# Hash attention and Fourier mixing on one core: values of pairs 5 to 15 fetched by GpSimd through a table of row numbers

## The chip, the core and the metric

The kernel runs on one core of one Trainium2 chip. The metric is the device time of one execution in microseconds. Names in the profile: PE is TensorE (matrix products), PEld its weight loads, DVE is VectorE, ACT is ScalarE, POOL is GpSimd and SP is SyncE, which here only issues DMA transfers. [...]

## The reference, cut to what matters

```python
# q, k, v: (4, 8, 768, 64) float32; proj: (64, 6)
q_bits = (einsum('bhsd,dk->bhsk', q, proj) > 0); k_bits likewise
mask = q_bucket[:, :, :, None] == k_bucket[:, :, None, :]     # buckets: 6 bits as a number
scores = where(mask, q @ k^T / 8, -1e9)
attn = softmax(scores)                                        # per batch and head, 768 x 768
x = (attn @ v) -> (B, S, H*D)                                 # (4, 768, 512)
u = x + real(fft(fft(x, axis=1), axis=2))
un = (u - mean(u)) / sqrt(var(u) + 1e-6)
out = u + relu(un @ w_ch1) @ w_ch2                            # 512 -> 2048 -> 512
```

## The kernel before, in words

There are 4 batches with 8 heads each. The heads are worked in pairs of two: pair n (0 to 15) holds heads 2t and 2t+1 of batch b, with n = 4b + t. Four constants are used below: P = 128 partitions, NT = 6 blocks of 128 rows in a sequence of 768, D = 64 and NPAIR = 4.

**Attention.** For each pair there are six steps, one per block c of 128 keys. In a step, weigh forms the transposed scores in PSUM (L893), ScalarE takes the exponential into the tile pk (L897), VectorE sets the pairs of different buckets to zero (L903) and adds up the denominators in acc (L988). One step later values multiplies by the values (L914): the weights loaded into TensorE are a block of 128 rows and 64 columns of vn, the tile of values of this pair. In vn (128 partitions, 768 columns) block c of head h stands in columns (2c + h) * 64 and up; partition p holds row 128c + p of the sequence. There are two such tiles in turn, so the values of pair n + 1 go where those of pair n - 1 were, and they can be fetched when the last product of pair n - 1 is done.

**Loads.** load(n) fetches q, k and v of a pair. It is called for pair n + 1 at the start of pair n, before the pair's first step. In the kernel before all of it is issued on SyncE's queue (for pair 0 partly on ScalarE's): for pairs 1 to 15, q takes 8 transfers, k takes 4 and v takes 2, one for each head (L562), each with 768 pieces of 256 bytes.

**Mixing.** mix(b) is the Fourier transform as products with constant tables (L1086, L1115), and then mlp7(b), the two linear layers with seven products in place of eight (L1390 for the first, L1270 for the second). The transposed u comes back through ScalarE (L1142); spread computes the mean and the variance of its rows on VectorE, and on GpSimd the scale rs (L1151 and L1152), with which VectorE later adds the second layer's products to the output (L1282). store sends the output from GpSimd's queue (L1024), for the last batch from SyncE's.

**Weights.** The weights come as 64-bit numbers and are made 32-bit on the chip by narrow, of which ScalarE does L647, L654 and L655, and VectorE L639, L643 and L652. The first layer's are fetched on SyncE's queue during batch 0. The second layer's are fetched on GpSimd's queue (L693, tile zraw) in 16 transfers of 512 KB into two buffers in turn, while the attention of batch 1 runs. From batch 1 on the first layer's blocks come back from a scratch tensor ad (L1363) and the second layer's from bd (L1275), on SyncE's queue.

**What sets the order.** Attention of batch b and the mixing of batch b - 1 are interleaved: after each step of attention(b) some steps of the generator mix(b - 1) are run. Up to the end of batch 0's attention the order of TensorE, VectorE, ScalarE and GpSimd is that of the program text (the block under tc.manual_schedule). From batch 1 on a planner sets the order on each engine: among the instructions whose operands are ready by its own modelled times it takes the one that stands earliest in the program, save for the chains of scores and values on TensorE, which behind() ties to each other with a higher rank. The load of pair 5 is called at the start of pair 4, which is the first pair of batch 1.

Of the kernel before, what the change touches and what calls it, by code (L numbers as in the profile page):

```python
# [13 lines left out]
I32 = mybir.dt.int32  # L14
# [6 lines left out]
P = 128  # L21
B, H, S, D = 4, 8, 768, 64
# [3 lines left out]
NT = S // P  # L26
NPAIR = H // 2
# [458 lines left out]
def _main(  # L486
# [13 lines left out]
    nc = tc.nc  # L500

    const = ctx.enter_context(tc.tile_pool(name="const", bufs=1))
# [11 lines left out]
    def wt(shape, dtype, tag, name, bufs=2):  # L514
        return work.tile(shape, dtype, tag=tag, name=name, bufs=bufs)
# [26 lines left out]
    def load(n, names="qkv", second=nc.sync):  # L542

        b, t = divmod(n, NPAIR)
        for nm in names:
            src = {"q": q, "k": k, "v": v}[nm]  # L550
            tag, bufs = ("vn", 2) if nm == "v" else ("qkn", 2)
            tl = wt([P, S], F32, tag, f"{nm}n{n}", bufs)
            nat[nm, n] = tl
            if nm == "v" or n == 0:
                tc_ = tl.rearrange("p (c h d) -> p c h d", c=NT, h=2)
                for h in range(2):
                    s = src[b, 2 * t + h]
                    s = (
                        s.rearrange("(p c) d -> p c d", c=NT) if nm == "q"
                        else s.rearrange("(c p) d -> p c d", p=P)  # L560
                    )
                    (second if h else nc.sync).dma_start(tc_[:, :, h, :], s)  # L562
                continue
            for i in range(4):
                s = src[b, 2 * t + i // 2, :, i % 2 * 32 : i % 2 * 32 + 32]
                d = tl[32 * i : 32 * i + 32]
                if nm == "k":
                    nc.sync.dma_start(
                        d.rearrange("p (j a) -> p j a", a=32),
                        s.rearrange("(j b) a -> b j a", b=32),  # L570
                    )
                else:
                    s = s.rearrange("(j b r) a -> r b j a", b=32, r=2)
                    d = d.rearrange("p (r j a) -> r p j a", r=2, a=32)
                    for r in range(2):
                        nc.sync.dma_start(d[r], s[r])

    load(0, "qk", nc.scalar)
    warm = const.tile([1, 1], F32, tag="warm", name="warm")
    nc.gpsimd.memset(warm, 0.0)  # L580
# [13 lines left out]
    own = const.tile([P, 2], F32, tag="own", name="own")  # L594
    nc.sync.dma_start(own, cn["own"].ap())
    load(0, "v")
    pj = const.tile([P, 32], F32, tag="pj", name="pj")
    nc.gpsimd.memset(pj, 0.0)
# [112 lines left out]
    def weights1():  # L711
# [11 lines left out]
        for i in range(arrival.depth):  # L723
            arrival.fetch(i)
            if i == 1:
                load(1)
# [826 lines left out]
def kernel(tc, *args):  # L1553

    cn = {n: tc.nc.inline_tensor(a, name="k_" + n) for n, a in _consts().items()}
    with ExitStack() as ctx:
        large = _main(ctx, tc, *args, cn)
    with tc.If(large > 0, preferred_fallthrough_block=False):
        _any_scores(tc, *args, cn)
# [34 lines left out]
```

## Time and profile before

| | |
|---|---|
| median of 2 runs | 1102.0 us (1101.22 to 1102.78) |
| the profiled execution | 1102.7 us, of which its span 1100.4 us |
| granted TensorE clock, mean | 0.994 |
| DMA: packets, bytes | 175,710, 103.13 MB |
| SyncE's hardware queue | 169,840 packets, 30.1% of 16 engines |
| GpSimd's software queue | 4,224 packets, 3.7% |
| instructions on GpSimd | 132 |

All times below are microseconds from the start of the span unless marked ns. A group row gives line, engine, operation, tiles (output <- inputs), number, busy time and mean. A row of waits gives who waited, for whom, the total time, how many times and the longest one. A row of a timeline gives start, duration, engine, line, operation and tiles, and in square brackets how long the engine had been idle and what ended this. DMA instructions on an engine's row last as long as the engine needs to issue them; the landing comes later, for vn 3.4 us (median) after the issue and for zraw fetches from GpSimd 4.0 us.

The attention of batch 0 takes the first 114 us or so; that of batch 1 lies between 124.8 and 447.9 us (first product of pair 4 to last of pair 7, with the mixing of batch 0 in between), batch 2 from there to 642.5, apart from an early start at 412.9, and batch 3 ends at 899.5. After that the rest of the mixing of batch 2 and that of batch 3 run alone.

### The profile page before, as it was taken

The numbers are of one execution on the slowest core, as the hardware profiler recorded it, in microseconds if no ns is written. First come the engines' busy times: TensorE is split into PE (matmuls) and PEld (weight loads), VectorE is DVE, ScalarE is ACT, GpSimd is POOL, SyncE is SP. The second block draws the span as 40 slices with busy tenths as digits, with TensorE's granted clock in tenths as the row PEclk, the third lists the DMA queues.
The fourth block names the chain that finished last, engine by engine and source line by source line (L and its number), as shares of the span: only waits on it lengthen the run. The fifth ranks groups of instructions, "written<-read, shape, count | busy, mean of one in ns | idle before, by whom it ended". The sixth has DMA issues, their size and how long they took to land.

```text
span 1100.4 us, 14144 instructions
## 1 busy us (share of the span) xinstructions
PE 1043.3 (95%) x4933; PEld 632.7 (57%) x4933; DVE 790.5 (72%) x1336; ACT 499.5 (45%) x1055; POOL 58.6 (5%) x132
## 2 busy tenths in 40 slices
PE   7989897999989999999999999999999999999996
PEld 3333353446744675545664576645674569768575
DVE  5899958878599977776767785965856785644353
ACT  6987555553276324454326433355315522340420
POOL 0000000002000020010000011001000002100000
PEclk9999999999999999999999999999999999999998
DMA  9755353451056161322154134213032205122301
GB/s 222 224 95 126 64 140 72 138 164 19 20 149 209 44 204 26 68 63 66 26 157 107 48 82 153 44 43 92 15 129 68 68 24 172 55 81 88 123 20 41
DMA packets 175710, 103.13 MB, mean 94 GB/s; under 512 B 129552, under 2 KB 162960, under 8 KB 175632
## 3 DMA queue, kind: packets, MB, share of 16 engines
q1 hardware_dynamic: 169840, 88.65, 30.1%
q0 software_dynamic: 4224, 13.11, 3.7%
q8 instruction: 41, 0.67, 0.2%
q10 hardware_dynamic: 1568, 0.39, 0.2%
q14 instruction: 37, 0.30, 0.1%
HBM read 81.14 MB, written 20.97 MB: 93 GB/s over the span
## 4 chain that ended last, share of the span: by engine, by line
PE 61%; DVE 11%; ACT 4%; DMA 2%; issue 2%; DVEq 0%; SPq 0%; ACTq 0%
PE o L1270 22%; PE h_p L1390 20%; PE oo L914 6%; PE sc L893 6%; DVE pk L903 3%; PE cs L1086 2%; DMA zraw<-in_moe_w_ch_dram 2%; PE A L1115 2%; PE B L1115 1%; DVE acc L988 1%; ACT rr L948 1%; DVE w L1282 1%; DVE h L1256 1%; PE bits L825 1%; PE un L1141 1%
## 5 line engine op out<-in xcount | busy, mean ns | idle before, releaser
L1270 PE MATMUL o<-w,h 128*128 128x256 f32 x1152 | 259.4, 382 | 1.2 <-ACT tq L1289 0.7
L1270 PEld LDWEIGHTS o<-w,h 128*128 128x128 f32 x1152 | 216.3, 190 | 43.6 <-issue 4.6
L897 ACT ACTIVATE pk<-sc 128x768 f32<-128x768 f32 x192 | 147.6, 809 | 78.4 <-PE sc L893 60.9
L1390 PE MATMUL h_p<-x,w 128*128 128x384 f32 x448 | 163.5, 495 | 3.2 <-ACT h L1412 1.5
L893 PE MATMUL sc<-qt,kt 64*128 64x384 f32 x768 | 155.7, 508 | 6.0 <-ACT pk L897 5.7
L914 PE MATMUL oo<-pk,vn 128*64 128x385 f32 (+1 forms) x768 | 155.3, 499 | 6.0 <-DVE pk L903 3.0
L903 DVE SCALAR_TENSOR_TENSOR pk<-qb,kb,pk 128x768 f32<-128x768 bf16 x132 | 129.0, 1012 | 30.2 <-ACT pk L897 30.1
L1390 PEld LDWEIGHTS h_p<-x,w 128*128 128x128 f32 x448 | 82.3, 190 | 71.0 <-ACT pk L897 5.4
L988 DVE TENSOR_TENSOR acc<-acc,pk 128x1536 f32<-128x1536 f32 (+1 forms) x72 | 105.7, 1482 | 7.2 <-ACT pk L897 6.7
L1390 PE MATMUL h_p<-w 128*128 128x384 f32 x288 | 105.5, 489 | 2.3 <-ACT w L1427 2.3
L914 PEld LDWEIGHTS oo<-pk,vn 128*64 128x64 f32 x768 | 49.1, 136 | 100.0 <-issue 69.3
L893 PEld LDWEIGHTS sc<-qt,kt 64*128 64x128 f32 x768 | 66.9, 188 | 51.3 <-issue 24.0
L1390 PEld LDWEIGHTS h_p<-w 128*128 128x128 f32 x288 | 53.7, 190 | 41.7 <-ACT w L1427 3.5
L1300 ACT COPY tq<-o 128x256 f32<-128x256 f32 x24 | 8.9, 372 | 105.1 <-PE o L1270 105.1
L1282 DVE SCALAR_TENSOR_TENSOR w<-o,rs,w 128x256 f32<-128x256 f32 x56 | 26.7, 478 | 41.6 <-PE o L1270 41.6
L1270 PE MATMUL o<-w 128*128 128x256 f32 x176 | 42.3, 383 | 1.3 <-DVE w L1282 1.3
L1416 DVE TENSOR_TENSOR h<-h 128x384 f32<-128x384 f32 x32 | 17.8, 556 | 33.1 <-ACT h L1415 33.1
L1289 ACT COPY tq<-o 128x256 f32<-128x256 f32 x24 | 8.9, 371 | 69.3 <-PE o L1270 69.2
L1270 PEld LDWEIGHTS o<-w 128*128 128x128 f32 x176 | 32.8, 190 | 8.8 <-DVE w L1282 2.9
L1423 DVE TENSOR_TENSOR h<-h 128x384 f32<-128x384 f32 x32 | 17.7, 553 | 27.0 <-ACT h L1422 27.0
L1024 POOL DMA_DIRECT2D out_dram<-w x30 | 16.4, 548 | 388.7 <-issue 293.2
L1086 PE MATMUL cs<-ch,z 128*128 128x128 f32 (+3 forms) x192 | 33.2, 324 | 3.0 <-DVE bt L829 1.9
(170 smaller groups left out, 1312.4 us busy)
## 6 DMA issues: line engine op xcount, KB each, us to landing
w<-ad SPq DMA_DIRECT2D x168, 128.0 KB, 2.0
w<-bd SPq DMA_DIRECT2D x42, 512.0 KB, 4.5
zraw<-in_moe_w_ch_dram POOLq DMA_DIRECT2D x16, 512.0 KB, 4.0
bd<-w SPq DMA_DIRECT2D x14, 512.0 KB, 3.9
vn<-in_v_dram SPq DMA_DIRECT2D x32, 192.0 KB, 3.4
qn<-in_q_dram SPq DMA_DIRECT2D x120, 48.0 KB, 2.4
kn<-in_k_dram SPq DMA_DIRECT2D x60, 96.0 KB, 3.4
zraw<-in_moe_w_ch_dram SPq DMA_DIRECT2D x8, 512.0 KB, 5.7
```

The costliest lines, as they stand in the source:

```text
L893: last[0] = nc.tensor.matmul(ps[:, h, 0:HALF], kt[rows, ks], qt[rows, qs], start=kb is not None, stop=True,)
L897: nc.scalar.activation(pk[:, g, :, 0:HALF], ps[:, :, 0:HALF], AF.Exp, scale=SCALE)
L903: nc.vector.scalar_tensor_tensor(w, qb[:, h].rearrange("p (g s) -> p g s", g=2), kb[:, h, c : c + 1], w, op0=ALU.is_equal, op1=ALU.mult,)
L914: nc.tensor.matmul(oos[g][h * D : (h + 1) * D, 0:w], nat["v", n][:, (2 * c + h) * D : (2 * c + h + 1) * D], pk[:, g, h, 0:w], start=(c == ...
L988: nc.vector.tensor_tensor(acc[:, g], (first if c == 1 else acc)[:, g], new[:, g], op=ALU.add,)
L1086: nc.tensor.matmul(ps[:, pc + 2 * lo : pc + 2 * hi - 1 : 2], z[:, cp, pc, par, t * P : (t + 1) * P], ch[:, cp, pc, lo:hi], start=(cp == 0) ...
L1115: nc.tensor.matmul(ps[:, cols], F[:, par, k, t, j * P : (j + 1) * P], sq[:, t, k, cols], start=(t == 0), stop=(t == 1),)
L1270: nc.tensor.matmul(ps, a[:, r], right7[i][:, r], start=start and r == 0, stop=r == HF // 2 - 1, skip_group_check=not start,)
L1282: nc.vector.scalar_tensor_tensor(t[:, cols], src, r, t[:, cols], op0=ALU.mult, op1=ALU.add)
L1390: nc.tensor.matmul(ps, left[:, k], right[i][:, k], start=start and k == 0, stop=k == 1, skip_group_check=not start,)
L1416: nc.vector.tensor_tensor(c21, c12, c21, op=ALU.add)
L1423: nc.vector.tensor_tensor(c22, c21, c22, op=ALU.add)
```

## The change

From pair 5 on (n > NPAIR) the values of a pair are no longer fetched by two transfers of SyncE. GpSimd issues twelve indirect transfers instead, one for each block c and head h. Each fetches 128 rows of 64 numbers; the row of v that goes to partition p is read from the column (2t + h) * 6 + c of a table rowid, to which the start of the batch is added as a constant. rowid has 128 partitions and 48 columns of 32-bit numbers; a single iota on GpSimd fills it at the start of the kernel, and column j holds 128j + p in partition p. So every row goes where it went before, and the rows are asked for in their old order. The loads of q and k, and of the values of pairs 0 to 4, stay.

```diff
             if nm == "v" or n == 0:
+                if n > NPAIR:
+                    rows = v.rearrange("b h s d -> (b h s) d")
+                    for j in range(2 * NT):
+                        c, h = divmod(j, 2)
+                        nc.gpsimd.indirect_dma_start(
+                            tl[:, j * D : (j + 1) * D], None, rows,
+                            bass.IndirectOffsetOnAxis(
+                                rowid[:, (2 * t + h) * NT + c : (2 * t + h) * NT + c + 1], 0
+                            ),
+                            element_offset=b * H * S * D,
+                        )
+                    continue
                 tc_ = tl.rearrange("p (c h d) -> p c h d", c=NT, h=2)
...
+    rowid = const.tile([P, H * NT], I32, tag="rowid", name="rowid")
+    nc.gpsimd.iota(rowid, pattern=[[P, H * NT]], base=0, channel_multiplier=1)
     load(0, "qk", nc.scalar)
     warm = const.tile([1, 1], F32, tag="warm", name="warm")
     nc.gpsimd.memset(warm, 0.0)
```

## The prediction, made before the result was known

> **What bounds the kernel now.** I read the page's busy table first, then the busy time by stage, then the waits of TensorE, then the transfers of values on SyncE's queue in order of time, and last the timeline of GpSimd around them.
>
> ```profile
> ## 1 busy us (share of the span) xinstructions
> PE 1043.3 (95%) x4933; PEld 632.7 (57%) x4933; DVE 790.5 (72%) x1336; ACT 499.5 (45%) x1055; POOL 58.6 (5%) x132
> ```
>
> TensorE is busy for 1043.3 of 1100.4 us, so all that any change can win is in the other 57 us; GpSimd is nearly empty. By stage (columns: stretch, its length, then the busy time of PE, PEld, DVE, ACT and POOL):
>
> ```profile
> 100.00:250.00 150.00, 131.79 (x647) 65.78 (x644) 119.65 (x215) 84.65 (x173) 5.57 (x10) 0.98 0.44 118
> 250.00:450.00 200.00, 191.06 (x907) 122.36 (x907) 166.59 (x294) 85.94 (x185) 18.93 (x35) 1.00 0.32 93
> 450.00:900.00 450.00, 443.96 (x2009) 262.16 (x2007) 324.80 (x493) 190.28 (x401) 19.66 (x43) 1.00 0.28 75
> ```
>
> Of TensorE's idle time 18 us lie between 100 and 250 us and 9 us in the next 200; from 450 to 900 us it is 98.7% busy. The first stretch is where a late operand shows at once. The waits of TensorE say what the idle time is for:
>
> ```profile
> PE sc L885 <- ACT pk L897: 6.0, 7, 1.9
> PE sc L893 <- ACT pk L897: 5.7, 3, 2.7
> PE trq L773 <- DMA qn<-in_q_dram: 5.0, 1, 5.0
> ```
>
> The only DMA wait of weight is the first load of q. No wait for vn, the tile of values, is in the list. SyncE's queue shows why (start, duration, instruction):
>
> ```profile
> 115.38 1.06 SPq L562 DMA_DIRECT2D vn<-in_v_dram  x2
> 159.42 0.97 SPq L562 DMA_DIRECT2D vn<-in_v_dram  x2
> 245.65 0.98 SPq L562 DMA_DIRECT2D vn<-in_v_dram  x2
> 317.67 1.79 SPq L562 DMA_DIRECT2D vn<-in_v_dram  x2
> ```
>
> These are the loads for pairs 5 to 8. Counting the products of L914 in the timeline (a pair has 24: six blocks of keys, two halves of the queries, two heads; each leaves two records), the first use comes at 164.4, 248.4, 321.0 and 412.9 us: 49, 89, 75 and 95 us after the issue; for pairs 9 to 15 it is 69 to 88 us. GpSimd's timeline at the same places:
>
> ```profile
> 161.55 0.54 POOL L693 DMA_DIRECT2D zraw<-in_moe_w_ch_dram  x1 [9.09 <-ACT pk L897]
> 163.68 0.53 POOL L693 DMA_DIRECT2D zraw<-in_moe_w_ch_dram  x1 [1.60 <-ACT zraw L655]
> ...
> 250.31 0.51 POOL L1151 TENSOR_SCALAR rs<-mv 128x1 f32<-128x1 f32 x2 [29.31 <-DVE mv L1149]
> 250.91 1.10 POOL L1152 TENSOR_TENSOR rs<-rs,mhalf 128x1 f32<-128x1 f32 x2
> ...
> 263.00 1.69 POOL L1151 TENSOR_SCALAR rs<-mv 128x1 f32<-128x1 f32 x1 [1.07 <-DVE mv L1149]
> ```
>
> Two fetches of raw weights follow the load of pair 6 by 2 and 4 us, and the row scales rs follow the load of pair 7 by 5 us. These are what the new transfers will stand in front of. The last line is the same instruction as in the first rs line (its median is 223 ns) and took 1.69 us: it ran while VectorE's acc sum (L988, 1.76 us from 262.85) held on.
>
> [...]
>
> **The change, part by part.**
>
> *Removed:* 22 of the 32 vn issues from SyncE, about 0.54 us each, so 12 us of its queue, and its waits for the buffer (vn behind "PE oo L914", 42.7 us in 9 waits in SyncE's own list). Behind them stand q, k and ad fetches. As TensorE waits for no DMA after the start, this is worth 0.
>
> *Added at the start:* one iota of 128x48 in front of GpSimd's memsets. It isn't in the trace; bounds are a memset of 128x32 (0.12 us) and the affine select of 128x128 (0.29 us). ident, which TensorE needs first, is ready at 1.4 us, and the q transfer holds TensorE to 5.9 us: 4 us of cover, cost 0. Without that cover it would be the 0.3 us.
>
> *Moved:* 11 loads of 12 indirect transfers, 132 instructions on GpSimd. The trace has no indirect transfer. Below, it can't be cheaper than a plain one on this engine (0.55 us, with no table to read); above, I take a plain one and one full lock-out like that of rs, 0.55 + 1.69 = 2.24 us. I use the middle, 1.4 us: 16.8 us a load (6.6 to 26.9), 185 us in all. Even then the values land some 20 us after the buffer is free and are wanted 49 to 95 us after: vn itself is late nowhere, cost 0. The rows and their 256 bytes are the same, so the traffic is too.
>
> What counts is what these 16.8 us stand in front of on GpSimd. From the second batch on the planner sets the order, and the load comes earlier in the program than the steps it collides with, so I put it first.
> - Pair 5 (115.4), 10, 11, 12, 14, 15: GpSimd has nothing else in those windows. 0.
> - Pair 6: 159.4 + 16.8 = 176.2. The fetches of 161.55 and 163.68 go 14.7 and 13.0 us later. ScalarE already waits for such fetches at L647 (2.0 and 3.7 us), and softmax exponentials queue behind. In the old order nearly all would reach TensorE; the planner knows that a load takes GpSimd's time and can put exponentials ahead of the conversion. Bounds 0 and 14.7; I take 3.
> - Pair 7: 245.6 + 16.8 = 262.4, then two rs pairs of 0.22 + 0.57 us: 264.0. VectorE's first sum with rs (L1282) starts at 261.4. 2.6 us late; I take 2 (0 at 0.55 us a transfer, 12.7 at 2.24).
> - Pair 8: 317.7 + 16.8 = 334.5, so the fetches of 322.8 and 327.6 are 11.7 and 7.4 us late; their weights are first used in the second outer product, from 364.8. I take 1 (0 to 12).
> - Pairs 9 and 13 (382.8 and 642.6): output stores wait up to 16.8 us. The next writers of those places are ad fetches whose products (L1390) start at 457.9, and ScalarE copies from 713.6 on. 0.
> - Waits: a pair's products now wait for 12 landings, not 2. A separate wait costs 0.05 us in TensorE's load queue at L914; 110 of them are at most 5.5 us, run ahead of a full engine. 0.
> - [...] while a load runs, VectorE is 84% busy (143.4 of 171.6 us over eleven windows of 15.6 us from each issue). If transfers only wait for it, as rs did, it loses nothing. 0; a rival has the other end.
>
> Sum: 3 + 2 + 1 = 6 us. The profiled execution took 1102.7 us, 2.3 of them around its span of 1100.4; the median of the runs is 1102.0. From the median: 1108 us.
>
> **Rivals.**
> [...] Against: in this trace GpSimd lost, and plain DMAs of GpSimd keep to 0.52 to 0.63 us. Price: if half of VectorE's 143.4 us in the windows is pushed back, 71.7 less its 28.2 us of idle time there: 43 us, 1145 us. It decides from 0.21 us of lock-out per transfer (28.2 / 132), and reaches 2% (22 us) at 0.38 us. This one ends slower.
>
> [...]
>
> *A better layout.* SyncE freed of its waits, and new places for steps in the 18 us of idle time before 250 us, a third of which could be won: 1096 us. Against: those idle times end with ScalarE and VectorE, not with DMA.
>
> *It does not move the work where it says:* if the transfers stood behind the stores that GpSimd waits for (141 us before 631.8), values would come late and TensorE would show waits for vn; the planner places by due time, so this is part of the slow cases.
>
> **How the numbers follow.** Likeliest, 1100 to 1122 us: 0.55. Better layout: 0.09. VectorE locked out, 1124 to 1165: 0.26. Slow descriptors or late values: 0.10. The range runs from 1097 to 1150; above it lie the slow descriptors (0.10) and a part of the lock case (about 0.05), below it some 0.04. Two per cent, 22 us, is about what a measurement of this kernel can tell from no change. Slower by more: the last two cases, 0.36. Faster by more: 0.02. Within: 0.62.
>
> **What would show it.** GpSimd should have some 265 instructions and 240 us busy; the software queue 21,120 packets (4,224 and 22 x 768), SyncE's 152,944. Right: indirect transfers of 1 to 2 us, no TensorE wait for vn, zraw and rs later by 10 us at 160 and 250 us, later stages unchanged. Wrong by the lock: L903 and L988 longer than 1012 and 1748 ns, or more VectorE idle in the windows. Wrong by slow descriptors: transfers over 3 us. The whole would fall if the planner lays out the second batch in another order.

## The result, and the profile after

The changed kernel takes 1135.2 us (median of 2 runs, 1134.91 to 1135.57) against 1102.0: a ratio of 1.0302 (95% interval 1.0257 to 1.0346), slower by more than 2%. The profiled execution took 1135.57 us, with a span of 1133.7 and a mean granted TensorE clock of 0.979 (0.994 before). The lines named here stand 14 further down in its profile: L893 is L907, L897 is L911, L903 is L917, L914 is L928, L988 is L1002, L1270 is L1284, L1282 is L1296, L1390 is L1404, L693 is L707, L647 is L661.

The busy table of the changed kernel, and three of its rows of groups and queues (group: busy time, mean ns, idle time before; queue: packets, MB, share of 16 engines):

```profile
PE 1054.2 (93%) x4933; PEld 638.8 (56%) x4933; DVE 791.2 (70%) x1336; ACT 500.4 (44%) x1055; POOL 216.9 (19%) x265
...
q0 software_dynamic: 8448, 17.45, 4.9%
...
L559 POOL DMA_INDIRECT vn<-in_v_dram,rowid x132 | 156.1, 1183 | 275.8 <-PE oo L928 238.1
...
L917 DVE SCALAR_TENSOR_TENSOR pk<-qb,kb,pk 128x768 f32<-128x768 bf16 x132 | 129.1, 1013 | 29.9 <-ACT pk L911 29.7
```

GpSimd has the 265 instructions, and an indirect transfer takes 1.18 us on it. VectorE's busy time is what it was (790.5 before), and its masking product too (1012 ns before). TensorE is busy for 10.9 us more, with the same number of instructions. So of 33.3 us more in the span, 10.9 are slower products and 22.4 idle time.

The same three stretches as before, with the same columns as in the prediction (PE, PEld, DVE, ACT and POOL busy, granted clock, DMA share, GB/s):

```profile
100.00:250.00 150.00, 129.34 (x624) 65.14 (x623) 114.49 (x205) 82.38 (x172) 32.87 (x35) 0.93 0.43 119
250.00:450.00 200.00, 176.47 (x791) 110.96 (x789) 151.34 (x277) 79.57 (x174) 61.49 (x71) 0.96 0.32 95
450.00:900.00 450.00, 440.70 (x2035) 261.02 (x2034) 327.76 (x493) 191.54 (x403) 107.00 (x113) 1.00 0.26 73
```

The third stretch is nearly untouched. In the second TensorE does 791 instructions in place of 907, and the granted clock, 1.00 before, is 0.96. The waits of TensorE name the places (total, times, longest):

```profile
PE h_p L1404 <- ACT h L1433: 10.6, 2, 9.5
PE sc L907 <- ACT pk L911: 7.6, 4, 5.7
PE o L1284 <- DVE w L1296: 7.3, 4, 6.0
```

None of the three is a wait for vn, and there is none of TensorE for vn in the whole list: the values are never late. Each of the three longest waits stands behind one load of values on GpSimd. For pair 8, first GpSimd's timeline of the changed kernel, then ScalarE's, then TensorE's:

```profile
337.34 1.14 POOL L559 DMA_INDIRECT vn<-in_v_dram,rowid  x1 [2.34 <-PE oo L928]
...
352.88 0.94 POOL L559 DMA_INDIRECT vn<-in_v_dram,rowid  x1 [0.30 <-issue]
353.81 1.19 POOL L707 DMA_DIRECT2D zraw<-in_moe_w_ch_dram  x2
```

```profile
357.78 0.69 ACT L661 ACTIVATE zraw<-zraw 128x512 int32<-128x512 uint32 x1 [10.90 <-DMA zraw<-in_moe_w_ch_dram]
358.37 0.46 ACT L1433 ACTIVATE h<-h_p 128x384 f32<-128x384 f32 x1
```

```profile
358.89 4.37 PE L1404 MATMUL h_p<-x,tq 128*128 128x384 f32 x8 [9.49 <-ACT h L1433]
```

The load began at 337.34. Its twelve transfers end at 353.8, and only then go the two fetches of raw weights that stood behind it. The first lands 4.0 us later. ScalarE's next instruction is the conversion of just these weights (L661); it has waited 10.9 us, and behind it in ScalarE's queue stands the activation h (L1433), for which TensorE waits. That h waits for nothing but its turn: TensorE's last product ahead of the wait ended at 349.4 us, 9 us before h. In the kernel before, the same conversion (L647 there) had waited 0.85 us:

```profile
327.60 0.67 ACT L647 ACTIVATE zraw<-zraw 128x512 int32<-128x512 uint32 x1 [0.85 <-DMA zraw<-in_moe_w_ch_dram]
```

Pair 6 goes the same way:

```profile
168.40 1.02 POOL L559 DMA_INDIRECT vn<-in_v_dram,rowid  x1 [0.30 <-PE A L1129]
...
170.96 0.60 POOL L707 DMA_DIRECT2D zraw<-in_moe_w_ch_dram  x1
...
185.42 0.58 POOL L707 DMA_DIRECT2D zraw<-in_moe_w_ch_dram  x1
```

```profile
189.43 0.65 ACT L661 ACTIVATE zraw<-zraw 128x512 int32<-128x512 uint32 x1 [11.52 <-DMA zraw<-in_moe_w_ch_dram]
```

```profile
192.93 2.93 PE L907 MATMUL sc<-qt,kt 64*128 64x384 f32 x8 [5.72 <-ACT pk L911]
```

Here the exponential pk (L911) stands behind the conversion, and TensorE waits 5.7 us for it. One fetch still goes out between the second and the third transfer; the one that stands behind all twelve is the next. In the kernel before that fetch went out at 175.14, and its conversion had waited 4.2 us:

```profile
179.06 0.70 ACT L647 ACTIVATE zraw<-zraw 128x512 int32<-128x512 uint32 x1 [4.22 <-DMA zraw<-in_moe_w_ch_dram]
```

For pair 7 it is the row scales:

```profile
257.94 1.44 POOL L559 DMA_INDIRECT vn<-in_v_dram,rowid  x1 [29.22 <-PE oo L928]
...
274.78 0.94 POOL L559 DMA_INDIRECT vn<-in_v_dram,rowid  x1 [0.30 <-issue]
275.79 0.53 POOL L1165 TENSOR_SCALAR rs<-mv 128x1 f32<-128x1 f32 x2
```

VectorE's queue stops for rs even ahead of the sums that use it, at the statistics of the next rows:

```profile
276.06 0.18 DVE L1163 BATCH_NORM_AGGREGATE mv<-bs 128x2 f32<-128x6 f32 x1 [6.17 <-POOL rs L1165]
```

Its first sum with rs (L1296) starts at 280.05 (261.41 before), and TensorE, which waits for this sum, goes on at 280.58 after 6.0 us:

```profile
280.58 3.41 PE L1284 MATMUL o<-w 128*128 128x256 f32 x8 [6.01 <-DVE w L1296]
```

Then there is a loss at the very start. SyncE's queue and TensorE's first product with pjw (a tile with the projection), in the kernel before and then in the changed one:

```profile
2.40 1.19 SPq L591 DMA_DIRECT2D pjw<-in_proj_dram  x2
```

```profile
8.38 1.51 PE L801 MATMUL bitsq<-qt,pjw 128*32 128x384 f32 x8
```

```profile
7.07 1.17 SPq L605 DMA_DIRECT2D pjw<-in_proj_dram  x2
```

```profile
12.09 1.58 PE L815 MATMUL bitsq<-qt,pjw 128*32 128x384 f32 x8 [3.27 <-DMA pjw<-in_proj_dram]
```

The iota at the head of GpSimd's queue moves the clearing of pjw from 0.90 to 1.13 us, and on SyncE's queue the fetch into the cleared tile now stands behind six other transfers (the small tables off and own, two of v and two of zraw).

Finally, what follows a stall. The changed kernel's stretches right behind the waits of pairs 6, 7 and 8 (columns as above):

```profile
192.90:196.00 3.10, 3.07 (x9) 1.40 (x10) 0.86 (x1) 2.94 (x10) 0.13 (x1) 0.50 0.64 174
280.50:284.10 3.60, 3.52 (x10) 2.65 (x12) 3.60 (x6) 0.07 (x1) 3.35 (x4) 0.58 0.00 0
358.80:363.30 4.50, 4.41 (x9) 2.62 (x10) 2.86 (x5) 2.29 (x7) 0.00 (x0) 0.65 0.00 0
```

The clock granted in these three stretches is 0.50, 0.58 and 0.65 of full speed. Eight products of scores take 2.93 us there in place of 1.56, eight of o 3.41 in place of 1.89, eight of h_p 4.37 in place of 2.74: each of these stalls, with waits of 5.7, 6.0 and 9.5 us, costs its wait and about 1.5 us more.

How far the same products stand behind those of the kernel before shows where the time goes. The columns e2 and e8 belong to experiments below (us):

| product | before, at | after | e2, iota late | e8, twelve plain transfers |
|---|---|---|---|---|
| first of values, pair 5 | 164.4 | +5.96 | +0.16 | -1.33 |
| first of layer 1, batch 0 | 191.2 | +8.68 | +2.99 | -6.62 |
| last of values, pair 5 | 245.1 | +12.04 | +6.43 | -3.58 |
| first of layer 1, second half | 302.0 | +19.73 | +14.16 | -3.60 |
| last of layer 1, second half | 364.2 | +30.74 | +25.17 | -3.66 |
| end of the span | 1100.4 | +33.3 | +26.6 | -3.9 |

From the column "after": start 6.0, pair 6 6.1, pair 7 7.7, pair 8 11.0, all that follows 2.6; together 33.3 us. From pair 9 on GpSimd has nothing urgent behind a load, and little is lost. The 6.1 us of pair 6 are not the price of its block alone. The planner changed TensorE's order too, and e8, which has the changed order but no long block, is 6.6 us ahead of the kernel before at the first product of layer 1 and only 3.6 us ahead at the last of values; in between it waits 3.60 us for an activation h. The changed kernel waits 3.75 us at the same product. So the price of the block is read from e2 against e8: 8.1 us at pair 6.

### The profile page after: what moved, and what is told of

It is laid out like the page before. It is cut to its first block, busy times and chain, and to the rows that moved or that the text cites. A ratio compares the mean times of both kernels' runs of the same rounds, so it can differ in the third digit from the quotient of the medians.

```text
span 1133.7 us, 14350 instructions
## 1 busy us (share of the span) xinstructions
PE 1054.2 (93%) x4933; PEld 638.8 (56%) x4933; DVE 791.2 (70%) x1336; ACT 500.4 (44%) x1055; POOL 216.9 (19%) x265
## 3 DMA queue, kind: packets, MB, share of 16 engines
q0 software_dynamic: 8448, 17.45, 4.9%
## 4 chain that ended last, share of the span: by engine, by line
PE 67%; DVE 14%; ACT 6%; DMA 5%; issue 4%; POOL 3%; SPq 1%; DVEq 0%; ACTq 0%; POOLq 0%
PE h_p L1404 22%; PE o L1284 21%; PE oo L928 8%; PE sc L907 7%; DMA zraw<-in_moe_w_ch_dram 3%; POOL vn L559 3%; DVE pk L917 2%; DVE acc L1002 2%; PE cs L1100 2%; PE A L1129 2%; ACT pk L911 1%; PE B L1129 1%; ACT rr L962 1%; DMA kn<-in_k_dram 1%; PE un L1155 1%
## 5 line engine op out<-in xcount | busy, mean ns | idle before, releaser
L1284 PE MATMUL o<-w,h 128*128 128x256 f32 x1152 | 259.4, 382 | 1.1 <-ACT tq L1303 0.8
L1284 PEld LDWEIGHTS o<-w,h 128*128 128x128 f32 x1152 | 216.3, 190 | 43.5 <-issue 4.6
L559 POOL DMA_INDIRECT vn<-in_v_dram,rowid x132 | 156.1, 1183 | 275.8 <-PE oo L928 238.1
L911 ACT ACTIVATE pk<-sc 128x768 f32<-128x768 f32 x192 | 148.2, 809 | 83.3 <-PE sc L907 67.2
L1404 PE MATMUL h_p<-x,w 128*128 128x384 f32 x448 | 163.5, 494 | 4.0 <-ACT h L1426 2.1
L907 PE MATMUL sc<-qt,kt 64*128 64x384 f32 x768 | 157.9, 515 | 7.6 <-ACT pk L911 7.6
L928 PE MATMUL oo<-pk,vn 128*64 128x385 f32 (+1 forms) x768 | 156.7, 504 | 6.7 <-DVE pk L917 3.7
L917 DVE SCALAR_TENSOR_TENSOR pk<-qb,kb,pk 128x768 f32<-128x768 bf16 x132 | 129.1, 1013 | 29.9 <-ACT pk L911 29.7
L1404 PEld LDWEIGHTS h_p<-x,w 128*128 128x128 f32 x448 | 82.1, 190 | 71.5 <-issue 6.8
L1002 DVE TENSOR_TENSOR acc<-acc,pk 128x1536 f32<-128x1536 f32 (+1 forms) x72 | 105.8, 1483 | 7.3 <-ACT pk L911 6.8
L1404 PE MATMUL h_p<-w 128*128 128x384 f32 x288 | 105.5, 489 | 2.3 <-ACT w L1441 2.3
L928 PEld LDWEIGHTS oo<-pk,vn 128*64 128x64 f32 x768 | 49.5, 137 | 101.3 <-issue 69.6
L907 PEld LDWEIGHTS sc<-qt,kt 64*128 64x128 f32 x768 | 68.5, 192 | 54.0 <-issue 25.3
L1404 PEld LDWEIGHTS h_p<-w 128*128 128x128 f32 x288 | 53.8, 190 | 41.7 <-ACT w L1441 3.5
L1314 ACT COPY tq<-o 128x256 f32<-128x256 f32 x24 | 8.9, 373 | 115.9 <-PE o L1284 115.9
L1296 DVE SCALAR_TENSOR_TENSOR w<-o,rs,w 128x256 f32<-128x256 f32 x56 | 26.8, 480 | 41.7 <-PE o L1284 39.6
L1284 PE MATMUL o<-w 128*128 128x256 f32 x176 | 43.8, 393 | 7.4 <-DVE w L1296 7.3
L1284 PEld LDWEIGHTS o<-w 128*128 128x128 f32 x176 | 33.7, 196 | 15.6 <-DVE w L1296 9.4
L1404 PE MATMUL h_p<-x,tq 128*128 128x384 f32 x64 | 25.7, 544 | 14.9 <-ACT h L1433 10.6
L1430 DVE TENSOR_TENSOR h<-h 128x384 f32<-128x384 f32 x32 | 17.8, 555 | 31.0 <-ACT h L1429 28.3
```

Of the source, the lines that this page charges most:

```text
L559: nc.gpsimd.indirect_dma_start(tl[:, j * D : (j + 1) * D], None, rows, bass.IndirectOffsetOnAxis(rowid[:, (2 * t + h) * NT + c : (2 * t + ...
L907: last[0] = nc.tensor.matmul(ps[:, h, 0:HALF], kt[rows, ks], qt[rows, qs], start=kb is not None, stop=True,)
L911: nc.scalar.activation(pk[:, g, :, 0:HALF], ps[:, :, 0:HALF], AF.Exp, scale=SCALE)
L917: nc.vector.scalar_tensor_tensor(w, qb[:, h].rearrange("p (g s) -> p g s", g=2), kb[:, h, c : c + 1], w, op0=ALU.is_equal, op1=ALU.mult,)
L928: nc.tensor.matmul(oos[g][h * D : (h + 1) * D, 0:w], nat["v", n][:, (2 * c + h) * D : (2 * c + h + 1) * D], pk[:, g, h, 0:w], start=(c == ...
L1002: nc.vector.tensor_tensor(acc[:, g], (first if c == 1 else acc)[:, g], new[:, g], op=ALU.add,)
```

## The experiments

Three theories stand behind the expectations. **Q**: the block of twelve transfers holds up what stands behind it on GpSimd's queue, and with that the engine whose next instruction waits for it; the iota does the same to pjw. **P**: each indirect transfer holds up VectorE. **L**: the planner lays the work out differently, and that layout costs.

**e1: the iota alone.** The table is built at the start as in the change, and no load uses it.

```diff
-                if n > NPAIR:
+                if n > NPAIR * B:        # never true: all values on SyncE
```

> The table is filled as in the change, but all values stay on SyncE. Theory Q (the loss comes from queue order: the twelve transfers stand in front of zraw fetches and row scales on GpSimd, and the iota moves the fetch of the projection pjw behind the values and two raw weights on SyncE): the whole start loss and nothing else, first product of values at about 21.5 us instead of 15.8, 1107 to 1108 us. Rival P [...]: nothing here, 1102. Rival L (the planner's other layout of batch 1 costs the time): 1102.

1107.91 us, ratio 1.005 (1.0031 to 1.0068). The first product of values starts at 21.07 (15.80 before), and the 5.3 us stay to the end. One iota, of 0.16 us in the changed kernel, costs over 5 us, with no load of values moved.

**e2: the change with the iota later.** It goes behind the last of the other memsets of the start, where the first products no longer depend on it.

```diff
-    rowid = const.tile([P, H * NT], I32, tag="rowid", name="rowid")
-    nc.gpsimd.iota(rowid, ...)
     load(0, "qk", nc.scalar)
...
+    rowid = const.tile([P, H * NT], I32, tag="rowid", name="rowid")
+    nc.gpsimd.iota(rowid, ...)
```

> The change in full, with the iota moved behind the other memsets of the start. Theory Q: the start is as before (first product at 15.8 us), all else as in the change: 1129 to 1130 us. If the iota has no part in the start loss: 1135.

1129.16 us, ratio 1.0246 (1.0228 to 1.0264). SyncE issues pjw at 2.39 us again and the start's loss is gone; those of pairs 6, 7 and 8 are all there (table above).

**e3: the same values from GpSimd in two plain transfers a pair.** No table.

```diff
+                    if n > NPAIR:
+                        nc.gpsimd.dma_start(tc_[:, :, h, :], s)
+                        continue
```

> No table and no indirect transfer: the two plain transfers of pairs 5 to 15 are issued by GpSimd instead of SyncE; TensorE's order is that of the change. A load holds GpSimd for about 1.1 us instead of 16. Theory Q: nothing of weight stands in front of zraw and rs any more, 1102 to 1105 us. Rival L: SyncE is as free and TensorE's order as changed as in the change, so the loss of batch 1 stays, about 1129 us. Rival P can't tell this one: no table is read, 1102 to 1105.

1101.32 us, ratio 0.9996 (0.998 to 1.0011). That GpSimd fetches the values costs nothing that can be measured, as long as it is quick.

**e4: the indirect transfers in threes.** All 132 are kept, the table too, but a load goes out in groups of three, at each of the next steps, and behind GpSimd's last zraw fetch, rs or store.

```diff
-                        nc.gpsimd.indirect_dma_start(
+                        parts.append(lambda ...: nc.gpsimd.indirect_dma_start(
...
+                    with tc.issue_after(behind_pool[0].ins) ...:
+                        for _ in range(3):
+                            if parts:
+                                parts.pop(0)()
```

> Iota late; all 132 indirect transfers as in the change, but traced three at a time after the pair's steps 1 to 4, each group behind the last zraw fetch, row scale or store of GpSimd that the program had issued by then. GpSimd's total time is the same. Theory Q: a fetch or scale waits for at most three or four transfers, some 4 to 5 us instead of 16: 1104 to 1112 us. Rival P: as many transfers beside as busy a VectorE, the loss of e2 stays, about 1129 us. Rival L: 1129 us.

1102.0 us, ratio 1.0009 (0.9993 to 1.0025). The group of transfers in this kernel, and GpSimd's timeline where rs of pair 7 is due:

```profile
L561 POOL DMA_INDIRECT vn<-in_v_dram,rowid x132 | 165.0, 1250 | 196.9 <-PE oo L933 158.7
```

```profile
260.82 2.35 POOL L561 DMA_INDIRECT vn<-in_v_dram,rowid  x1 [0.30 <-issue]
263.24 0.79 POOL L1180 TENSOR_SCALAR rs<-mv 128x1 f32<-128x1 f32 x1
```

The rs goes in between, behind three transfers and not twelve. The transfers are even a little dearer (1.25 us), and the loss is gone. So it is not what they cost but what stands behind them. Theory P falls here: the same number of transfers, beside a VectorE with the same instructions in the same order, cost the kernel nothing that shows.

**e5 and e6: the zraw fetches on SyncE.** e6 is the kernel before with its zraw fetches on SyncE's queue, e5 is e2 with the same edit.

```diff
-        arrival = Arrival(slices, [...], NDC * DFF // WC, nc.gpsimd)
+        arrival = Arrival(slices, [...], NDC * DFF // WC, nc.sync)
```

> As e2 (the change, iota late), but the sixteen fetches of the second layer's raw weights (zraw) are issued by SyncE, so that no transfer of values stands in front of them; the row scales stay behind the load of pair 7. Theory Q: of e2's 27 us the two losses at the zraw fetches (6.3 and 11.0 us in its trace) go and the 7.7 us at the row scales stay: 1109 to 1114 us. If the loss is not at those fetches: 1129.

> The kernel before, with nothing but its zraw fetches moved to SyncE: the control for e5. All theories: about as before, 1099 to 1106 us.

e6: 1096.14 us, ratio 0.9949 (0.9926 to 0.9973), faster than expected; the gain, 5.2 us between 164 and 243 us, I did not follow up. e5: 1102.81 us, ratio 1.0007 (0.9992 to 1.0022), below what was expected; its own control, e6, is faster than was assumed. What counts is e5 against e6: 6.7 us. In the profiled executions e5 stands 1.1 us ahead of e6 at the end of pair 5 and 8.0 us behind it from the first half of layer 2 on. All of that comes up at one product of layer 2, as a wait for the sum with rs:

```profile
261.59 3.78 PE L1285 MATMUL o<-w 128*128 128x256 f32 x8 [6.01 <-DVE w L1297]
```

With zraw out of GpSimd's queue the losses of pairs 6 and 8 are gone, and that of pair 7, where rs waits, is left: each of these losses belongs to what stands behind that block.

**e7 and e11: one pair alone.** The iota late, and only pair 7, or only pair 8, fetched with the table.

```diff
-                if n > NPAIR:
+                if n == 7:               # e11: n == 8
```

> Iota late, and of all pairs only pair 7's values come by the twelve indirect transfers; TensorE's and VectorE's orders are those of the kernel before. Theory Q: the row scales alone are late, 7.7 us as in e2's trace between the first of L1270 and the next L1390: 1108 to 1110 us. Rival P (a cost per transfer, 27 us over 132): 12 transfers cost 2.4 us, 1103 to 1105.

> The table is built late and the values of pair 8 alone are fetched with the table, those of all other pairs by SyncE as before. Theory Q (the block of twelve holds back the zraw fetch behind it): the loss of the changed kernel between the first and the last product of hp01 comes back alone, some 11 us, so 1110 to 1116 with the median of before at 1102; nothing is lost ahead of 302 us, and the fetch of zraw that stood at 317 us or so in before is issued only behind the twelfth transfer. Against it: if the 11.0 us were only the sequel of the two earlier losses (products that had slipped against the fetches), the time is 1102 to 1106. A gain of the planner's layout of up to 3 us may be taken off in both.

e7: 1110.07 us, ratio 1.0074 (1.0048 to 1.0101). Its products move from 1.3 us ahead of the kernel before to 7.5 us behind it, all in the first half of layer 2, from the products at 262.37 us of the kernel before on: 8.8 us. e11: 1113.17 us, ratio 1.0097 (1.0075 to 1.012). The shift is +0.44 to the end of pair 6 and +10.98 at the last product of that half. GpSimd's timeline of e11, then TensorE's:

```profile
333.58 0.95 POOL L559 DMA_INDIRECT vn<-in_v_dram,rowid  x1 [0.30 <-issue]
334.53 1.17 POOL L708 DMA_DIRECT2D zraw<-in_moe_w_ch_dram  x2
```

```profile
339.60 4.40 PE L1405 MATMUL h_p<-x,tq 128*128 128x384 f32 x8 [9.49 <-ACT h L1434]
```

It is the wait of the changed kernel, 9.49 us to the digit, without the losses of pairs 6 and 7 ahead of it. So the losses of pairs 7 and 8 come back alone, at about their size in e2. Pair 6 alone was not run.

**e8: twelve plain transfers a load.** The same blocks of 128 rows, and the same place in GpSimd's order as in e2; the table is missing.

```diff
-                        nc.gpsimd.indirect_dma_start(tl[...], None, rows, ...)
+                        r0 = (b * H + 2 * t + h) * S + c * P
+                        nc.gpsimd.dma_start(tl[:, j * D : (j + 1) * D], rows[r0 : r0 + P])
```

> In place of the twelve indirect transfers of a pair twelve plain ones of the same 128 rows, from GpSimd, with no table; all engines stand in the order of e2. Plain ones take 0.55 us each there: a load holds GpSimd for some 6.6 us, or 10 us if the 0.3 us between indirect transfers comes with plain ones too. Theory Q with the time in front of zraw and rs as the cause: pair 7 none to 2 us, the two zraw places some 1 to 4 us each: 1103 to 1111 us. If the number of transfers counts and not their length: 1129.

1100.66 us, ratio 0.9992 (0.9978 to 1.0007), better than expected. GpSimd's timeline at pair 7:

```profile
242.34 6.33 POOL L560 DMA_DIRECT2D vn<-in_v_dram  x12 [28.05 <-PE oo L922]
248.74 0.51 POOL L1159 TENSOR_SCALAR rs<-mv 128x1 f32<-128x1 f32 x2
```

A plain transfer takes 0.54 us and the next follows at once, so the block is 6.3 us long and not 17. This stays hidden. TensorE's instructions are in the same order in e2, e3, e4 and e8. It differs from that of before at 60 of 4,933 places, all between 182 and 228 us of the kernel before. So theory L falls as well: with this order the span of the profiled execution is 2.6 us shorter in e3 and 3.9 in e8, which the timed ratios don't tell from nothing. What e2 loses against e8 is the price of the block's length: by the table 8.1 us up to the first product of layer 1, then 7.8 and 11.1.

**e9, e10 and e12: can both edits be had at once?** e9 is e4 with zraw on SyncE, e10 is e3 with zraw on SyncE, e12 is e9 once more.

> e4 and e6 together: all 132 indirect transfers, iota late, three at a time between the row scales, and the zraw fetches on SyncE. Nothing is left that a load of values holds up for long. Theory Q: the gain of e6 (0.5%) with no loss beside it, 1094 to 1100 us against some 1102. If indirect transfers cost something besides their place in the queue, it shows here as the difference to e6.

> e3 and e6 together: the two plain transfers of values of pairs 5 to 15 on GpSimd, the zraw fetches on SyncE, no table. Theory Q: the two queues have changed places and neither holds up the other; 1092 to 1100 us, the gain of e6 or a little more. If e6's gain came from SyncE's queue as it was, with the values in it: 1100 or over.

> The kernel of e9 once more. In e9's profiled execution TensorE, VectorE, ScalarE and SyncE all stood still from about 591 to 595 us (ScalarE 4.47 us ahead of a product of scores that had been done for 2 us, VectorE 4.75, SyncE's queue 7.7), while GpSimd's transfers went on. If this belongs to the program (its orders, its twelve transfers of pair 11 just there), it returns at the same products and the profiled run is again near 1103. If it is an event of single executions, it is gone or elsewhere, and a run without it ends near 1096 to 1098.

e10: 1094.61 us, ratio 0.9923 (0.9901 to 0.9946): faster than both kernels, though its interval overlaps with that of e6. e9 missed what was expected: 1103.63 us, ratio 1.0011 (0.9998 to 1.0024). In its profiled execution 6.9 us are lost between 560 and 622 us. ScalarE's and VectorE's timelines there:

```profile
594.78 0.81 ACT L916 ACTIVATE pk<-sc 128x768 f32<-128x768 f32 x1 [4.47 <-remote]
```

```profile
595.62 1.95 DVE L922 SCALAR_TENSOR_TENSOR pk<-qb,kb,pk 128x768 f32<-128x768 bf16 x2 [4.75 <-issue]
```

TensorE and SyncE stood still over the same 4 us, while GpSimd's transfers went on. In e12, one execution of 1091.69 us, there is no such stop. So it is not a fixed part of the program. The stop is not the whole difference either: of the 11.6 us between the two profiled executions 6.1 lie at it and about 3 near 125 us. The 20 timed executions of e9 ran from 1099.15 to 1108.24, and what held them up is not known: whether the threes with zraw on SyncE are as good as e10 stays open.

## Why the prediction was right or wrong

The forecast was 1108, with a range of 1097 to 1150; 1135.2 lies in the range, 27 us above the likeliest value, and outside the 1100 to 1122 of its own case. That the range holds the result is luck: its part above 1122 was there for a VectorE held up by the transfers, and that did not occur. What was right is the kind of mechanism, a block on GpSimd's queue in front of zraw and rs; what was wrong is how much of it reaches TensorE. Step by step:

- **Removed work and vn itself, 0:** right. No wait of TensorE for vn, and e3 is the same as before.
- **The iota, 0 with 4 us of cover:** wrong, 5.7 us at the first product of values, 5.3 with the iota alone (e1). The step looked only at ident behind the iota. Behind it also stood the clearing of pjw, and the place of its fetch on SyncE's queue changed with the place of the iota (e1, e2).
- **1.4 us a transfer, 16.8 a load:** nearly right. 1.18 us and 0.30 us between two make loads of 16.5 to 17.8 us for pairs 6 to 8. The 0.30 us were not foreseen; they do not occur between plain transfers (e8).
- **Pair 6, 3 us:** 6.1 measured, 8 against the same order with plain transfers (e8). The mechanism was the one described, a conversion with exponentials behind it, but at another fetch. Of the two that were named, one went out ahead of the load and one after two transfers, in e2 at 161.8 and 165.2 us (161.55 and 163.68 before); the third, at 170.99 in e8, went at 179.6 in e2. That the planner would put them ahead of the conversion, the reason for taking 3 out of 0 to 14.7, did not happen.
- **Pair 7, 2 us:** 7.7. The rs came about as late as computed (17.8 us behind the load's start, 16.8 forecast). But the lateness was set against one sum alone, at 2.6 us. VectorE stopped earlier in its queue, at statistics that waited 6.17 us for rs, and had h and pk to do after them before the sum; TensorE waited 6.0 us, and its products then took 1.5 us more.
- **Pair 8, 1 us:** 11.0, the largest error. The delay of the fetches was right (11.7 us in e11, from 322.8 to 334.53), the user was not: I looked for the first product with these weights, from 364.8 us on, and not for the conversion that waits for them in ScalarE's queue, with TensorE's next operand directly behind.
- **Pairs 9 to 15, 12 waits, VectorE, 0:** right within the 2.6 us that are left over.
- **Traffic:** 8,448 packets in the software queue, not 21,120. The 16,896 added rows of 256 bytes went in 4,224 packets, four to a packet.
- **No price for a stall beyond its wait:** missing. TensorE's products were priced at full clock; 10.9 us of the 33.3 are the same products running longer, some 4.5 of them behind the three long waits.

Of the rivals, a VectorE held up by the transfers would have given 1145, near the result, and is refuted: VectorE's instructions kept their durations (the masking products 1,013 ns in the mean against 1,012 before, the sums of L1002 1,748 in the median in both), and the transfers took longer beside it, as rs did in the kernel before (1.69 us against a median of 0.22). Of the 132, 88 started while VectorE ran a TENSOR_TENSOR or SCALAR_TENSOR_TENSOR instruction, and took 1.29 us in the mean, 2.42 at the most; the other 44 took 0.96 in the mean. VectorE shows no loss: 28 of its 132 masking products (L917) started while an indirect transfer was running, and took 1,009 ns in the mean, against 1,014 for the 96 that met none. The case called slow descriptors in the forecast, transfers of over 3 us, is refuted too: in the changed kernel they took from 0.94 to 2.42 us. The better layout shows only in the spans of e3 and e8, by 2.6 and 3.9 us where the rival assumed 6; their timed ratios include 1. The failing steps are thus two: the sizing of the three delays, at 6 us together where the upper bounds added up to 39.4 and 24.8 were measured (8.1, 7.8 and 11.1 against the same order in e8); and the iota, at 0.

## What to carry to other kernels

When instructions are moved to an engine that looks empty, list what stands behind them on that queue within the length of the moved block, and for each follow the queue of the engine that waits for it: at pair 8 it was the next instruction in ScalarE's queue that counted, with 9.5 us of TensorE's time behind it, not the first user of the data. If a block of 17 us can be split and put behind the urgent instructions, as in e4, it need not cost anything: e4's ratio is 0.9993 to 1.0025. Each of the three stalls of TensorE from 5.7 us up cost about 1.5 us on top of its wait.

## What the runs showed that I had not expected

- Between indirect transfers GpSimd pauses for 0.30 us; between plain ones it does not (e8): 17 us against 6.3 for the same 12 blocks of 128 rows.
- At the start, after a wait of 3.27 us, groups of four products of scores took 1.49 us in place of 0.8 to 1.0, from 16.0 to 20.4 us, while the recorded clock of that stretch is 1.00. Why the record does not show it is open.
- An instruction of 0.16 us on an empty engine cost over 5 us: with it at the head of the queue, a transfer on another queue stood later.
